# A convolution by two-stage transforms and an MLP on one core: first inverse stage in 64x32 tiles, its shuffles to 32 partitions, four rows with the last pair read in place, filter chunk on other partitions, new order

## The chip, the core and the metric

The kernel runs on one core of one Trainium2 chip. A core has TensorE (PE in the profile; its weight loads are PEld), VectorE (DVE), ScalarE (ACT), GpSimd (POOL), SyncE (SP), which here only issues DMAs, and 16 DMA engines. The metric is the device time of one execution in microseconds; lower is better.

## What is computed

The input is x = A_q, 2048 positions by 448 channels in bfloat16. Two sublayers follow each other, each on a layer norm and with a residual. Cut to what matters:

```python
def _A_ref(q, k, v, shift_k, ssm_k, ssm_D):
    k_shift = sum(k_pad[:, t:t + S, :] * shift_k[:, ks - 1 - t] for t in range(ks))   # 4 taps
    kv = k_shift * v
    y = irfft(rfft(kv, padded to 2 * S) * rfft(ssm_k, padded to 2 * S))[:S]           # along positions
    return q * (y + kv * ssm_D)

def _B_ref(x, w1, b1, w2, b2):
    h = _layernorm(x)
    u = _gelu(einsum("bsd,sf->bdf", h, w1) + b1)      # mixes the 2048 positions
    return (einsum("bdf,fs->bds", u, w2) + b2).transpose(0, 2, 1)

h = x + _A_ref(_layernorm(x), A_k, A_v, ...)
out = h + _B_ref(_layernorm(h), B_w1, B_b1, B_w2, B_b2)
```

## The kernel before

Everything lies in one SBUF array, `arena`; the parts of it are reused from stage to stage. Position 16 q + r is kept on partition q in row r, so a tensor is 128 partitions by 16 rows by 448 channels. The long convolution is a transform of 4096 points in two stages forward, a product, and two stages back, each stage a set of small matmuls with constant tables.

The steps are named in the order table: *loads* and *con* (inputs and tables), *kT* (the filter, which comes as channels by positions in four chunks of 128, 128, 128 and 64 channels, is transposed on TensorE, line 1086), *kv* (transposes of k, line 988, the four-tap filter as matmuls with diagonal weights, line 1014, and the product with v on VectorE, line 1053), *k1* and *u1* (first forward stage of the filter and of kv, line 1114, four tiles of 32 columns; each result goes from PSUM to SBUF on ScalarE or VectorE, line 1130, and two of them are then shuffled from SBUF to SBUF by a DMA, line 1134), *k2* and *u2* (second forward stage, line 1154), *i1* (products and first inverse stage), *i2* (second inverse stage, line 1324, with the gate, the residual and the layer norm of each row), *mlp* (lines 1455, 1465 and 1476), and fillers on TensorE (*dummy*, *warm*, line 1235). *q* and *xn* are the first layer norm's statistics.

The forward tables of the second stage, FW, are made on GpSimd: four operations of line 888, each over the whole table, spread one small table (c_fw) by a mask. GpSimd also casts the taps (line 968) and makes the diagonal weights DG from them (line 973). A k2 or u2 matmul needs all four spreads.

The inverse stage works in eight pairs jj. VectorE makes two products of 128 by 1792 (line 1183) into a ring of four buffers. For each half h of the pair 16 matmuls of 64 by 64 tiles (line 1200) fill two PSUM banks, and as soon as a half is done its evacuation (line 797 on ScalarE) brings it to TU. Then two shuffles (line 1225) bring the pair to TZ, where each lands on 16 partitions in steps of eight:

```python
TZ[jj:jj + 121:8, 8 * s:8 * s + 8].rearrange("p r c d -> p r (c d)")   # <- TU[:, 2 * jj + s]
```

The order of the pairs is 6, 0, 1, 5, 4, 2, 3, 7. The last pair's shuffles are smaller (lines 1212 and 1218, two of them issued by GpSimd), because rows 0 and 1 read that pair in TU itself: the constant NZ is 2, their place in TZ is filled with zeros (line 1166, a DMA), and each has two more matmuls with a table EW (line 1330). All other rows wait for the last pair's shuffles.

The order of every engine's instructions is written out in the table ORDER, a string per engine of steps and numbers of operations in them; a planner in the kernel walks through it, gives out PSUM banks and sets semaphores. An engine runs its list strictly in order: what waits holds up all that is behind it. SyncE's list is the order of the DMAs on its queue.

## Time and profile before

| | |
|---|---|
| runs | 175.47 us median of 3 (174.85 to 177.84) |
| profiled execution | 176.85 us, its span 174.8 us |
| granted TensorE clock, mean | 0.99 |
| busy: PE, DVE, ACT, POOL | 161.4, 91.6, 84.4, 36.5 us |
| moved by DMA | 36.87 MB, 211 GB/s on average |

The span is what the trace covers, from the first to the last instruction; the rest of the execution's time lies around it. The page lists busy times, the chain of work that ended last, and groups of instructions by line. A row of the timeline gives start, length, engine, line, operation, shapes and count, and in brackets the idle time before it with what ended it. A row of the chain gives start, length and what. In the rows of DMA issues the last number is the time from issue to landing in microseconds. Stages, by the timeline: filter transposes 4.7 to 11.9, k1 from 12.3, taps 23.9 to 33.8, second stage from 35.5, products 53.3 to 72.2, first inverse stage to 73.3, second inverse stage from 77.3, MLP from 84.4 to the end.

### The profile page before, as it was taken

The numbers are of one execution on the slowest core, as the hardware profiler recorded it, in microseconds if no ns is written. First come the engines' busy times: TensorE is split into PE (matmuls) and PEld (weight loads), VectorE is DVE, ScalarE is ACT, GpSimd is POOL, SyncE is SP. The second block draws the span as 40 slices with busy tenths as digits, with TensorE's granted clock in tenths as the row PEclk, the third lists the DMA queues.
The fourth block names the chain that finished last, engine by engine and source line by source line (L and its number), as shares of the span: only waits on it lengthen the run. The fifth ranks groups of instructions, "written<-read, shape, count | busy, mean of one in ns | idle before, by whom it ended". The sixth has DMA issues, their size and how long they took to land.

```text
span 174.8 us, 3713 instructions
## 1 busy us (share of the span) xinstructions
PE 161.4 (92%) x1565; PEld 95.8 (55%) x1565; DVE 91.6 (52%) x170; ACT 84.4 (48%) x128; POOL 36.5 (21%) x67
## 2 busy tenths in 40 slices
PE   6889999879977899949999999999999999999994
PEld 2666886533323444413444555555567777777783
DVE  0249889969987999938888730000002232231232
ACT  3239994869987999953968522622120000000000
POOL 1006917900000000234588750000000000000000
PEclk9999999999999999987999999999999999999999
DMA  5999989977885569895999999960000111101111
GB/s 184 283 324 407 366 265 306 401 204 286 291 302 164 194 190 213 220 193 94 385 389 406 416 420 424 413 273 0 0 0 4 53 53 53 42 14 53 53 53 53
DMA packets 16702, 36.87 MB, mean 211 GB/s; under 512 B 2349, under 2 KB 10206, under 8 KB 16686
## 3 DMA queue, kind: packets, MB, share of 16 engines
q1 hardware_dynamic: 16446, 36.47, 61.4%
q8 instruction: 12, 0.20, 0.5%
q0 software_dynamic: 96, 0.09, 0.3%
q10 hardware_dynamic: 144, 0.08, 0.2%
q14 instruction: 4, 0.03, 0.1%
HBM read 23.79 MB, written 1.84 MB: 147 GB/s over the span
## 4 chain that ended last, share of the span: by engine, by line
PE 71%; DMA 15%; ACT 7%; DVE 3%; SPq 2%; issue 1%; DVEq 0%
PE ps L1476 24%; PE ps L1455 12%; PE ps L1465 12%; DMA arena<-arena 11%; PE ps L1200 7%; PE ps L1114 5%; DMA arena<-in_A_ssm_k_dram 4%; PE ps L1324 3%; DVE arena L1183 2%; ACT arena L1130 2%; PE ps L988 2%; ACT arena L798 2%; PE ps L1014 2%; ACT arena L797 2%; PE ps L1154 2%; SPq L872 1%
## 5 line engine op out<-in xcount | busy, mean ns | idle before, releaser
L1476 PE MATMUL ps<-arena 128*128 128x448 bf16 (+2 forms) x238 | 42.7, 342 | 0.0
L1479 DVE SCALAR_TENSOR_TENSOR arena<-ps,arena 128x448 bf16<-128x448 f32 (+2 forms) x17 | 11.2, 657 | 57.5 <-PE ps L1476 57.4
L1476 PEld LDWEIGHTS ps<-arena 128*128 128x128 bf16 x238 | 33.3, 145 | 9.5
L797 ACT CAST arena<-ps 128x896 bf16<-128x896 f32 (+1 forms) x28 | 22.7, 921 | 1.8 <-PE ps L1154 1.7
L1130 ACT CAST arena<-ps 128x896 bf16<-128x896 f32 (+2 forms) x27 | 21.4, 843 | 4.2 <-PE ps L1114 4.0
L1455 PE MATMUL ps<-arena 128*128 128x448 bf16 x112 | 22.5, 353 | 0.0
L1465 PE MATMUL ps<-arena 128*128 128x448 bf16 x112 | 21.4, 352 | 0.0
L1154 PE MATMUL ps<-arena 128*64 128x448 bf16 x128 | 15.0, 359 | 3.7 <-DMA arena<-arena 2.0
L1445 ACT ACTIVATE arena<-ps,arena 128x448 bf16<-128x448 f32 x14 | 8.1, 643 | 20.5 <-PE ps L1465 14.3
L1183 DVE TENSOR_TENSOR arena<-arena 128x1792 bf16<-128x1792 bf16 x16 | 16.5, 1086 | 1.7 <-DMA arena<-arena 1.6
L1114 PE MATMUL ps<-arena 128*32 128x448 bf16 (+2 forms) x288 | 16.3, 335 | 0.4 <-ACT arena L798 0.3
L1455 PEld LDWEIGHTS ps<-arena 128*128 128x128 bf16 x112 | 10.7, 98 | 10.8 <-DVE arena L1408 1.0
L1465 PEld LDWEIGHTS ps<-arena 128*128 128x128 bf16 x112 | 11.0, 98 | 10.2
L1200 PE MATMUL ps<-arena 64*64 64x448 bf16 x256 | 13.7, 353 | 1.0 <-DVE arena L1183 0.5
L888 POOL TENSOR_SCALAR arena<-arena 128x1024 f16<-128x1024 f16 x4 | 11.4, 2851 | 13.3 <-DMA arena<-c_fw 13.3
L1154 PEld LDWEIGHTS ps<-arena 128*64 128x64 f16 x128 | 5.6, 108 | 12.4 <-ACT arena L797 2.8
L1200 PEld LDWEIGHTS ps<-arena 64*64 64x64 f16 x256 | 7.0, 106 | 7.3 <-ACT arena L797 3.1
L1324 PE MATMUL ps<-arena 128*128 128x448 bf16 x32 | 8.5, 375 | 2.6 <-DMA arena<-arena 2.5
L1269 POOL TENSOR_SCALAR arena<-arena 128x4 f32<-128x4 f32 (+1 forms) x5 | 1.3, 266 | 45.4 <-DVE arena L1263 45.3
L800 DVE COPY arena<-ps 128x1024 bf16<-128x1024 bf16 (+1 forms) x10 | 6.3, 654 | 8.0 <-PE ps L1086 8.0
L1114 PEld LDWEIGHTS ps<-arena 128*32 128x32 f16 x288 | 7.3, 95 | 5.5 <-ACT arena L798 1.5
L1378 ACT ACTIVATE arena<-arena 128x448 bf16<-128x448 bf16 x14 | 8.0, 572 | 4.2 <-DVE arena L1349 3.9
(61 smaller groups left out, 170.9 us busy)
## 6 DMA issues: line engine op xcount, KB each, us to landing
arena<-arena SPq DMA_DIRECT2D x16, 448.0 KB, 5.3
arena<-in_B_w_dram SPq DMA_DIRECT2D x8, 896.0 KB, 10.1
arena<-in_B_w_dram SPq DMA_DIRECT2D x2, 2048.0 KB, 17.5
arena<-arena SPq DMA_DIRECT2D x14, 224.0 KB, 4.2
arena<-in_B_w_dram SPq DMA_DIRECT2D x2, 1536.0 KB, 19.3
arena<-in_A_k_dram SPq DMA_DIRECT2D x4, 448.0 KB, 7.5
arena<-in_A_q_dram SPq DMA_DIRECT2D x4, 448.0 KB, 5.8
arena<-in_A_v_dram SPq DMA_DIRECT2D x4, 448.0 KB, 8.8
```

The source lines that it names most:

```text
L797: return e.copy(out=dst(), in_=src())
L888: return e.tensor_scalar(out=dst, in0=FC, scalar1=MK[:, k:k + 1], scalar2=None, op0=ALU.mult)
L1114: op("pe", lambda e, W, quad=quad, r=r, q=q, x=x, c0=c0, d0=d0, dw=dw: e.matmul(quad(x, q), E0[:, 128 * x + c0:128 * x + c0 + 32], src[:, ...
L1130: return e.copy(out=dst, in_=u) if W == "act" else e.tensor_copy(out=dst, in_=u)
L1154: op("pe", lambda e, W, b=bs[h], h=h, j=j, c=c, par=par: e.matmul(PS[64 * par:64 * par + 64, b.slots[c], 0:D], FW[:, 2 * j + h, 64 * c:64 ...
L1183: op("dve", lambda e, W, m=m, i=i: e.tensor_tensor(out=MR(m.slots[0]).rearrange("p (x y) d -> p x y d", x=2), in0=TU[:, i].unsqueeze(2).br ...
L1200: k = op("pe", lambda e, W, b=bs[h], m=ms[h], par=par, t=t, tab=tab, xy=xy, s=s, o=o: e.matmul(PS[64 * o:64 * o + 64, b.slots[s], 0:D], ta ...
L1324: k = op("pe", lambda e, W, b=b, r=r, h=h: e.matmul(Pb(b), ET[:, 2 * r + h, :], TZ[:, slot[r], h, :], start=(h == 0), stop=(h == 1 and r > ...
L1455: op("pe", lambda e, W, r=r, fc=fc, b=bs[fc]: e.matmul(Pb(b), W1A[:, r, 128 * fc:128 * fc + 128], Q[:, r, :], start=(r == 0), stop=(r == R ...
L1465: op("pe", lambda e, W, r=r, fc=fc, b=b: e.matmul(Pb(b), W1B[:, r, 128 * (fc - n0):128 * (fc - n0) + 128], Q[:, r, :], start=(r == 0), sto ...
L1476: op("pe", lambda e, W, r=r, fc=fc, b=b, d0=d0, d1=d1: e.matmul(Pb(b)[:, d0:d1], W2[fc // 7][:, fc % 7, r:S:R], G[:, fc, d0:d1], start=(fc ...
L1479: op("dve", lambda e, W, r=r, b=b, d0=d0, d1=d1: e.scalar_tensor_tensor(out=X[:, r, d0:d1], in0=Pb(b)[:, d0:d1], scalar=bm[:, r:r + 1], in ...
```

## The change

**First inverse stage.** The tiles are 64 rows by 32 columns: 64 matmuls a pair instead of 32, each with 32 columns of weights, and the two halves of a pair meet in the same four PSUM banks. So both evacuations of a pair follow its last matmul. A bank now holds, in its four partition quarters, the four sums of the pair for the same rows, and a shuffle lands on 32 partitions in steps of four:

```diff
-                        for s, par in ((0, 0), (0, 1), (1, 0), (1, 1)):
-                            o = par ^ s
-                            k = op("pe", lambda e, W, b=bs[h], m=ms[h], par=par, t=t, tab=tab, xy=xy, s=s, o=o: e.matmul(
-                                PS[64 * o:64 * o + 64, b.slots[s], 0:D], tab[64 * par:64 * par + 64, 64 * s:64 * s + 64],
...
+                        for g in range(4):
+                            for par in range(2):
+                                qd = (2 * h + par) ^ g
...
+                                    PS[32 * qd:32 * qd + 32, bs[g >> 1].slots[g & 1], 0:D],
+                                    tab[64 * par:64 * par + 64, 32 * g:32 * g + 32],
...
-                        TZ[jj:jj + 121:8, 8 * s:8 * s + 8].rearrange("p r c d -> p r (c d)"),
-                        TU[:, 2 * jj + s].rearrange("p c d -> p (c d)")),
...
+                            TZ[off:off + 125:4, c, 8 * g:8 * g + 8].rearrange("p (a b) d -> p a (b d)", b=2), view(o_u, [2 * D])),
```

Here c is jj >> 2 and off is jj & 3; TZ has its two halves apart (`[2, R, D]` instead of `[R, 2, D]`). The table for this stage is half as large.

**Last pair.** Rows 0 to 3 (NZ is 4) read it in TU, with one more matmul each. Its first shuffle carries rows 4 to 7 alone (128 runs of 896 bytes), its second is whole; both are issued by SyncE. The zeros are written by GpSimd (line 1155 of the changed kernel) and not by a DMA. Rows 4 to 7 wait for the first of the two shuffles, rows 8 to 15 for the second.

```diff
-                        for h in range(2):
-                            k = op("pe", lambda e, W, b=b, r=r, h=h: e.matmul(
-                                Pb(b), EW[:, 2 * r + h, :], TU[:, R - 1, h, :], start=False, stop=(h == 1)),
...
+                        k = op("pe", lambda e, W, b=b, r=r: e.matmul(
+                            Pb(b), EW[:, r, :], view(o_TU + (4 * (R // 2 - 1)) * DB, [D]), start=False, stop=True),
```

**Filter.** The chunk of 64 channels is loaded to partitions 32 to 95 instead of 0 to 63, into a buffer that VectorE fills with zeros before, and is transposed like the others with 128 rows. The load waits for the fill.

```diff
+            op("dve", lambda e, W: e.memset(KN[:, 3, :], 0.0), w=[(o_KN + 4096 * 3, 4096)], est=620.0)
...
-                op(Dq, lambda e, W, c=c: e.dma_start(KN[0:CW[c], c, :], A_ssm_k[128 * c:128 * c + CW[c], :]),
...
+                op(Dq, lambda e, W, c=c: e.dma_start(KN[KP[c]:KP[c] + CW[c], c, :], A_ssm_k[128 * c:128 * c + CW[c], :]),
```

**Gate.** The gate's value of rows 4 and up is written to the ring of product buffers instead of over TZ.

**Order.** ORDER is new for all engines. Of one engine's string, as an example, three rows of SyncE's:

```diff
-        "xload.3:0 i1.14:36 i1.14:35 i1.1:36 i1.1:35 i1.4:35 i1.4:34 i1.12:35-36 i1.10:36 i1.10:35 i1.6:36 i1.6:35 "
...
+        "i1.1:67-68 i1.14:67-68 i1.8:68 i1.8:67 i1.10:68 con.8:0 i1.10:67 i1.12:67-68 i1.6:67-68 i1.4:66-67 w1a.0:0 "
+        "i1.16:67-68 w1a.1:0 w1a.2:0 w1a.3:0 w1b.0:0-3 w2.0:0-3 mlp.25:15 mlp.27:15 mlp.29:15 mlp.31:15 mlp.33:15 "
```

The pairs come as 0, 6, 3, 4, 5, 2, 1, 7. Lines are those of each kernel: the changed kernel's 900, 860, 911, 921, 918, 906, 903, 928 and 914 are loads (filter, constants, k, biases, D, taps twice, x, v).

SyncE at the start, of the changed kernel, from the fourth DMA on; ahead of it are one filter chunk, the identity and the 64-channel chunk.

```order
L900 DMA arena<-in_A_ssm_k_dram 128x2048 x2
L911 DMA arena<-in_A_k_dram 128x1792
L921 DMA arena<-in_B_b_dram 14x128
L860 DMA arena<-c_e 128x256
L860 DMA arena<-c_fw 128x1032
L918 DMA arena<-in_A_ssm_D_dram 1x448
L911 DMA arena<-in_A_k_dram 128x1792 x2
L906 DMA arena<-in_A_shift_k_dram 64x4
L911 DMA arena<-in_A_k_dram 128x1792
L903 DMA arena<-in_A_shift_k_dram 128x3x4
L928 DMA arena<-in_A_q_dram 128x1792
L906 DMA arena<-in_A_shift_k_dram 64x4
```

The 64-channel chunk has moved from behind the other three to ahead of two of them; c_fw stands before most of k instead of behind the first x load; the last piece of the taps (the second row of 906) stands behind all of k and one load of x.

GpSimd before, from the first table spread (line 888) on, and then the same place of the changed kernel (spread 876, cast of the taps 960, diagonal weights 965, zeros 1155; 1269 and 1254 belong to the layer norm and wait for VectorE):

```order
L888 TENSOR_SCALAR arena<-arena 128x64x16
L968 CAST arena<-arena 128x16
L973 TENSOR_TENSOR arena<-arena 128x1024
L888 TENSOR_SCALAR arena<-arena 128x64x16
L1269 TENSOR_SCALAR arena<-arena 128x2
L888 TENSOR_SCALAR arena<-arena 128x64x16
```

```order
L960 CAST arena<-arena 128x16
L876 ISA
L876 TENSOR_SCALAR arena<-arena 128x64x16
L965 TENSOR_TENSOR arena<-arena 128x1024
L876 TENSOR_SCALAR arena<-arena 128x64x16 x2
L1236 MEMSET arena 128x2
L876 TENSOR_SCALAR arena<-arena 128x64x16
L1155 MEMSET arena 128x4x448
```

The cast now stands ahead of the first spread, and the layer norm's operations behind the last. On TensorE the first k2 group comes, before, when all of line 1014 is done; in the changed kernel four k2 groups stand behind the fourth of its eight steps and after the last k1 group.

SyncE at the end of the inverse stage, before and then changed (1225 and 1209 are shuffles of pairs, 1212, 1218 and 1204 smaller ones of the last pair, 1428 and 1413 quarters of the first half of W1, 860 and 872 tables):

```order
L1428 DMA arena<-in_B_w_dram 128x4x896
L1166 DMA arena<-arena 16x4x448
L936 DMA arena<-in_A_q_dram 128x1792
L1225 DMA arena<-arena 16x8x896 x14
L1212 DMA arena<-arena 16x8x448 x2
L1218 DMA arena<-arena 8x6x448 x2
L872 DMA arena<-c_et 128x1024
```

```order
L1209 DMA arena<-arena 32x4x896 x7
L860 DMA arena<-c_ew 128x512
L1209 DMA arena<-arena 32x4x896 x7
L1413 DMA arena<-in_B_w_dram 128x4x896
L1204 DMA arena<-arena 32x4x448
L1209 DMA arena<-arena 32x4x896
L1413 DMA arena<-in_B_w_dram 128x4x896 x3
```

The first quarter of W1 has moved from ahead of all inverse shuffles to between pair 1 and the last pair, 7.

TensorE in the second inverse stage of the changed kernel (1220 warm, 1310 the stage's two matmuls a row, 1315 the in-place ones, 1440 MLP): the nine matmuls up to the second 1315 need nothing of the last pair's shuffles; the next, row 7's second one, does.

```order
L1220 MATMUL ps<-arena 128x448
L1310 MATMUL ps<-arena 128x448 x2
L1315 MATMUL ps<-arena 128x448
L1310 MATMUL ps<-arena 128x448 x5
L1315 MATMUL ps<-arena 128x448
L1310 MATMUL ps<-arena 128x448
L1315 MATMUL ps<-arena 128x448
L1310 MATMUL ps<-arena 128x448 x7
L1220 MATMUL ps<-arena 128x448
L1315 MATMUL ps<-arena 128x448
```

Before, rows 0 and 1 came first with four matmuls each, and all others behind the last pair's shuffles.

130 lines of the change are left out of this document (58 added, 72 removed), and 103 rows, old and new, of the table ORDER.

## Prediction

> **What bounds the kernel now.** I read the page's engine shares first, then the chain of waits in order of time, then the stretches of the windows view in which the chain stands on a DMA.
>
> ```profile
> PE 161.4 (92%) x1565; PEld 95.8 (55%) x1565; DVE 91.6 (52%) x170; ACT 84.4 (48%) x128; POOL 36.5 (21%) x67
> ```
>
> TensorE is busy for 92% of the span, but that is a mean over three parts. The chain shows them:
>
> ```profile
> 3.83 6.81 DMA arena<-in_A_ssm_k_dram
> ...
> 10.69 1.18 PE ps L1086 x16
> ...
> 23.97 2.39 PE ps L1014 x74
> ...
> 47.14 6.11 DMA arena<-arena
> ...
> 53.33 1.10 DVE arena L1183
> ...
> 74.30 6.35 DMA arena<-arena
> ...
> 80.70 0.75 PE ps L1324 x2
> ```
>
> From 80.70 on TensorE hardly stops (the 84 to 104 row below is 20.00 of 20), and the change leaves that work as it is: whatever makes it run through earlier than 80.70 comes off the end one for one. Before it there are three places where something else is last: the filter's last chunk (landing at 10.64), the last forward shuffle (landing at 53.25, and VectorE's first product behind it), and the last inverse shuffle (landing at 80.65). In the windows view (engine columns, granted clock, DMA share, GB/s) the first and the third look alike:
>
> ```profile
> 8.00:10.00 2.00, 1.22 (x16) 1.08 (x16) 0.00 (x0) 0.60 (x2) 0.00 (x0) 1.00 1.00 196
> 14.00:20.00 6.00, 6.00 (x138) 4.46 (x138) 5.95 (x13) 5.69 (x9) 5.24 (x4) 1.00 1.02 410
> 65.00:68.00 3.00, 3.00 (x60) 1.48 (x54) 3.00 (x4) 3.00 (x5) 0.00 (x0) 1.00 0.97 206
> 73.00:79.00 6.00, 3.73 (x19) 1.57 (x16) 3.24 (x9) 3.81 (x7) 2.40 (x3) 0.89 1.11 199
> 78.00:81.00 3.00, 2.76 (x8) 0.89 (x7) 1.77 (x4) 0.00 (x0) 1.28 (x2) 0.50 0.73 119
> 84.00:104.00 20.00, 20.00 (x106) 9.81 (x105) 15.01 (x47) 12.84 (x35) 15.18 (x38) 1.00 1.05 405
> ```
>
> The DMA engines are busy throughout (share about 1) yet move 196 to 206 GB/s while the 64-partition filter chunk or the inverse shuffles run, against 405 to 410 elsewhere. Half the rate is lost where few partitions are written.
>
> **The change part by part**, in times of the profiled execution.
>
> *Filter chunk.* It now lands on partitions 32 to 95 and is third in the queue. The filter and the identity are 1.88 MB; the queue had moved about 0.25 MB at 3.0, so at 400 GB/s the rest is through at 7.1 and landed at 8.2. Sixteen transposes of 1.18 us and the evacuation behind them: k1 can start at about 10; before, it came behind the transposes that ended at 11.87. The chunk has to wait for its zero fill, and with it SyncE and every load behind it.
>
> ```profile
> L1063 DVE MEMSET arena<- 128x448 bf16 x1 | 0.4, 432 | 0.9 <-PEq L1524 0.9
> ```
>
> The fill of 2048 columns starts behind this one at 1.3 and takes between 0.5 us (hardly more than for 448) and 2.0 (in proportion). The load would go out at 1.6; up to 1.4 us of delay lie behind the 524 KB already queued, so 0 to 0.8 us are left: I take 0.2. From there to the first filter-gate matmul (L1014 at 23.97) TensorE was busy without a gap (the 14 to 20 row) and has the same work less one k1 group: 21.7. Term: −2.3 us.
>
> *Where that lead goes.* The new order puts four k2 groups on TensorE right behind k1's last group, ahead of half the L1014 matmuls. k2 needs all four table spreads of GpSimd:
>
> ```profile
> 14.67 2.85 POOL L888 TENSOR_SCALAR arena<-arena 128x1024 f16<-128x1024 f16 x1 [13.32 <-DMA arena<-c_fw]
> 17.48 0.19 POOL L968 CAST arena<-arena 128x16 f32<-128x16 bf16 x1
> 17.76 1.90 POOL L973 TENSOR_TENSOR arena<-arena 128x1024 bf16<-128x1024 bf16 x1
> 32.35 2.86 POOL L888 TENSOR_SCALAR arena<-arena 128x1024 f16<-128x1024 f16 x1
> 35.47 0.95 PE L1154 MATMUL ps<-arena 128*64 128x448 bf16 x8 [1.16 <-POOL arena L1281]
> 7.74 0.47 SPq L914 DMA_DIRECT2D arena<-in_A_shift_k_dram  x1
> arena<-in_A_shift_k_dram SPq DMA_DIRECT2D x1, 0.5 KB, 7.0
> ```
>
> Before, the fourth spread ended at 35.2, since VectorE's statistics stood between them, and TensorE waited 1.16 us for it (the row names the small operation just behind it). Now the four follow each other, but the L968 cast stands ahead of all of them, and it needs the last shift-filter piece. Before, that landed at 14.7 (issued at 7.74, 7.0 us), behind some 3.6 MB; now it is behind 4.5 MB, at full rate about 15.2. So 15.2 + 0.2 + 4 × 2.85 + 1.9 + 0.3 = 29.0. TensorE gets to k2 after half of L1014 (208 matmuls at 2.39 us for 74, so 3.4 us), two k1 groups and a warm matmul: 21.7 + 4.5 = 26.2. It waits 2.8 us, and the rest of L1014 waits behind it, with VectorE's multiplies and nearly all of ScalarE's evacuations behind that. From 29.0 ScalarE has 20 evacuations to the last u1 group.
>
> ```profile
> 45.75 0.90 ACT L1130 CAST arena<-ps 128x896 bf16<-128x896 f32 x1
> 54.29 19.92 ACT L797 CAST arena<-ps 128x896 bf16<-128x896 f32 x24 [1.23 <-PE ps L1154]
> 70.08 2.08 DVE L1183 TENSOR_TENSOR arena<-arena 128x1792 bf16<-128x1792 bf16 x2
> arena<-arena SPq DMA_DIRECT2D x4, 448.0 KB, 3.1
> ```
>
> At 19.92/24 = 0.83 us each, and 0.7 us to the first, that is 46.3, with some waiting 46.8; before it was 46.65. The lead is used up: +0.1, between −1.5 (the piece lands at 13.5) and +1.5.
>
> *First product.* Before, the last u1 shuffle shared the queue with its neighbour and a table (6.11 us). Now ScalarE does two k2 evacuations and one of u1 between them, so it should land in 3 to 4 us (3.1 for one in an emptier queue). Then VectorE decides: four to five evacuations at 1.04 us stand ahead of the product, 51.6 against 53.33. Term, from 46.65: −1.8 us in all, from 0 to −3.
>
> *Products and first inverse stage.* On VectorE 16 products at 1.03 and two evacuations follow in both kernels: 18.8 us, last product at P = 70.4 instead of 72.16. TensorE has 512 matmuls of 32 columns instead of 256 of 64:
>
> ```profile
> 59.70 3.22 PE L1200 MATMUL ps<-arena 64*64 64x448 bf16 x64 [0.49 <-DVE arena L1183]
> ```
>
> Four tiles side by side ran at 50 ns a matmul. If eight run side by side, it is 25 ns, and a pair of products takes 1.6 us as before, under the 2.08 that VectorE needs. The L1014 row shows 32 ns a matmul, weights included, so such a pace can be issued; from 25 to 32 the cost is 0 to 0.3 us at the end. I take 0.
>
> *The tail.* The pair's two evacuations now both wait for its last matmul: they end at P + 0.2 + 0.8 (32 matmuls) + 0.25 + 2 × 0.83 = P + 2.9 instead of about P + 2.05 (the shuffle of 74.30 follows them), which costs 0.85. Against this the shuffles write 32 partitions. Stage 1 shuffles of that pattern are part of the 410 GB/s row, so the backlog at half rate (73 to 79) should go. The Trainium skill, page "SBUF — State Buffer", section "Door 1: The DMA port swizzle", says that bits 2 to 4 and 6 of the partition choose the port: by that, steps of eight or partitions 0 to 63 reach 8 of 16 ports, and steps of four or 32 to 95 reach all. The slow rows agree; by the page the new rate would be double, no run here shows it yet.
>
> But the first quarter of W1 (896 KB) now stands on SyncE ahead of the last pair's two shuffles. What an 896 KB load does to a small transfer behind it, one place shows:
>
> ```profile
> 53.27 0.39 SPq L1428 DMA_DIRECT2D arena<-in_B_w_dram  x1
> 53.70 0.66 SPq L1166 DMA_DIRECT2D arena<-arena  x1
> arena<-in_B_w_dram SPq DMA_DIRECT2D x1, 896.0 KB, 4.9
> arena<-arena SPq DMA_DIRECT2D x1, 56.0 KB, 4.8
> arena<-arena SPq DMA_DIRECT2D x2, 224.0 KB, 3.3
> ```
>
> The 56 KB landed 0.3 us after the load. So: the pair before ends its evacuations at P + 0.85, its second shuffle takes SyncE half a microsecond, the load is issued at P + 1.45 and lands at P + 6.35, and the first piece of the last pair at P + 6.7, the second at P + 7.2; before, TensorE went on at 80.70 = P + 8.54. Rows 0 to 3 need only the shuffle before that, at P + 3.0, right behind the nine warm matmuls; nine of their matmuls run before TensorE stops at row 7. Term: −1.8 us. Bounds: +0.4 with a backlog as before, −3.5 if the last pair isn't held up (3.3 us from its issue at P + 2.2).
>
> *After that:*
>
> ```profile
> 77.28 0.57 PE L1324 MATMUL ps<-arena 128*128 128x448 bf16 x2 [2.27 <-DMA arena<-arena]
> 84.39 1.11 PE L1455 MATMUL ps<-arena 128*128 128x448 bf16 x5
> ```
>
> 17 matmuls stand between TensorE's restart and the first MLP matmul (L1455), against 17 before in 84.39 − 80.70 = 3.7 us, the first of them at half clock: −0.2, if VectorE's queue (rows 2 and 3 are combined before row 0 is normalised) isn't later than TensorE.
>
> **Sum:** −1.8 (first product) − 1.8 (tail) − 0.2 = −3.8 us: span 171.0. The profiled execution took 176.85 for its span of 174.8; the runs shown have a median of 175.47, and I take the difference from that: **171.7 us**, by itself 169 to 174.
>
> **Rivals.**
>
> *The last pair isn't held by the W1 load* (0.18). For it: shuffles of 224 KB landed in 3.3 us. Against: the 56 KB row. Then TensorE hardly stops: −1.7 more, 170.0.
>
> *The lead is lost in idle stretches* (0.25). TensorE now stands idle about 2.8 us at k2 and 1.8 us before row 7. After the 2.3 us idle before 77.3 the clock was 0.50 for 3 us (the 78 to 81 row); there a DMA was last anyway. Once after k2 it costs 1.5 us, and the table pieces may land 1 us later: 174.1. The same if the shuffles stay near 200 GB/s, with the W1 load on top of their backlog: 174. Against: 1.5 us gaps elsewhere left the clock at 1.00.
>
> *Eight tiles don't run side by side* (0.17). If the two row halves take turns, the pace stays 50 ns: 512 matmuls are 25.6 us, from 4.5 us after the first product, and the stage ends 30.1 us after it instead of 19.8: +10.3, 182.0. TensorE decides from (19.8 − 4.5)/512 = 30 ns on; at 37 ns all of the gain is gone, at 44 the kernel is 2% slower. Against it: four tiles already share banks in pairs at 50 ns. The Trainium skill, page "TensorEngine Tiling (Array Packing)", section "Restrictions and Gotchas", says that different row tiles cannot access the same PSUM bank at the same time. By that rule the pace would be this rival's; but the 64x64 tiles also write one bank from both row halves, and at 50 ns for 448 columns they do not take turns, so the trace speaks against it.
>
> **How the numbers follow.** The forecast has 0.40, the first rival 0.18: faster by over 2% (about what a measurement of this kernel can tell from no change) 0.58; within 2% 0.25; slower 0.17. The range for 8 in 10 takes in the first two rivals with the bounds of the front, and the third up to 41 ns: 168.0 to 177.5.
>
> **What would show it.** Right: filter transposes over by 10; a TensorE wait on GpSimd of 2 to 3 us before k2 near 26 to 29; last product near 70; DMA near 400 GB/s in the inverse stage; the first MLP matmul near 80.5. Wrong: L1189 matmuls above 30 ns, the last shuffle landing over 7.5 us behind the last product, or a clock of 0.50 after k2.

## The result, and the profile after

The changed kernel is slower: 181.24 us median (179.44 to 181.38) against 175.16 for the kernel before, ratio 1.034 (95% interval 1.025 to 1.043). The forecast had 171.7 us, with 177.5 at the upper end of its range. The profiled execution took 181.38 us for a span of 179.4.

The chain of waits of the changed kernel in order of time (start, length, what):

```profile
8.80 6.29 DMA arena<-in_A_shift_k_dram
15.09 0.03 POOLq L558
15.12 1.72 issue
...
17.12 2.86 POOL arena L876
...
21.86 5.65 POOL arena L876 x2
...
27.55 2.83 POOL arena L876
...
30.73 1.70 PE ps L1144 x8
...
50.11 5.22 DMA arena<-arena
...
55.35 1.09 DVE arena L1170
...
68.92 0.43 PE ps L1189 x8
69.36 1.71 ACT arena L795 x2
...
79.02 4.99 DMA arena<-arena
```

Where the kernel before had the filter's chunk and TensorE's own work at the front, GpSimd's table spreads now stand on the chain up to 30.4. What holds them up is the last piece of the taps. The chain puts the end of GpSimd's wait down to another piece (landing at 15.09) and calls the rest "issue", but the small cast behind it waits for three pieces. The last went out at 9.97, and the slower of line 906's two pieces took 6.8 us:

```profile
9.97 0.47 SPq L906 DMA_DIRECT2D arena<-in_A_shift_k_dram  x1
DMA to landing us min/median/max: 6.2/6.5/6.8
```

So it landed at 16.81 (the trace has the last sixteenth of it there), and GpSimd went on at 16.86. In the inverse stage TensorE and ScalarE take turns. The last shuffle (79.02) still ends it, in 5.0 us instead of 6.4.

The timeline of the same kernel shows what each place costs:

```profile
21.96 1.62 PE L1006 MATMUL ps<-arena 64*128 64x256 bf16 x44 [0.19 <-issue]
30.73 1.70 PE L1144 MATMUL ps<-arena 128*64 128x448 bf16 x8 [3.77 <-POOL arena L876]
32.47 1.73 ACT L796 ACTIVATE arena<-ps 128x896 bf16<-128x896 f32 x2 [5.05 <-PE ps L1144]
34.12 1.29 DVE L1045 TENSOR_TENSOR arena<-ps,arena 128x512 bf16<-128x512 f32 x2 [5.15 <-PE ps L1006]
69.34 1.71 ACT L795 CAST arena<-ps 128x896 bf16<-128x896 f32 x2 [0.47 <-PE ps L1189]
71.53 1.71 ACT L795 CAST arena<-ps 128x896 bf16<-128x896 f32 x2 [0.47 <-PE ps L1189]
78.09 1.71 ACT L795 CAST arena<-ps 128x896 bf16<-128x896 f32 x2 [0.47 <-PE ps L1220]
84.06 0.36 PE L1310 MATMUL ps<-arena 128*128 128x448 bf16 x1 [2.49 <-DMA arena<-arena]
88.97 1.31 PE L1440 MATMUL ps<-arena 128*128 128x448 bf16 x5
```

The filter gate starts at 21.96, 2.0 us ahead of before (forecast 21.7). Then TensorE stands 3.77 us in front of k2, and ScalarE and VectorE over 5. In the inverse stage a pair of evacuations comes every 2.19 us, each time after 0.47 us of waiting; before, 24 evacuations followed each other without a gap (the row of 54.29 in the prediction). The first MLP matmul comes at 88.97 instead of 84.39.

The windows of the changed kernel (engine columns, granted clock, DMA share, GB/s):

```profile
31.00:36.00 5.00, 5.00 (x80) 3.04 (x80) 1.37 (x3) 2.78 (x4) 0.00 (x0) 0.74 0.43 150
81.00:84.00 3.00, 0.57 (x3) 0.10 (x1) 1.55 (x4) 0.83 (x3) 0.00 (x0) 1.00 0.97 355
84.00:88.00 4.00, 3.94 (x13) 1.75 (x14) 1.60 (x5) 2.63 (x5) 0.55 (x1) 0.60 0.55 157
```

The clock is 0.74 behind the wait at k2 and 0.60 behind the wait at 84. These are means over the windows: in the trace's record of the clock it is 0.50 from 30.19 to 33.60 and from 84.80 to 88.21, and 1.00 around that. The 355 GB/s are of W1 and the last pair together; what the new placement does to the shuffles alone, e5 shows below.

In every run of this study the part from the first MLP matmul to the end takes 90.2 to 90.5 us. So a run is three lengths: up to the first product, from there to the end of the last inverse evacuation (the stage), and from there to the first MLP matmul (the tail). All times are from the timelines; ratios are to runs of the kernel before of the same series, with 95% intervals. They leave out runs over 1.5% above the fastest of the same kernel, so that e2's rests on three of ten runs, e5's on two of four, and e16 with one run left has none; the profiled executions of these three are among those left out.

| run | ratio | first product | stage | tail | first MLP |
|---|---|---|---|---|---|
| before | 1 | 53.33 | 20.9 | 10.2 | 84.39 |
| forecast | | 51.6 | 21.7 | 7.3 | 80.6 |
| changed | 1.034 (1.025 to 1.043) | 55.35 | 24.5 | 9.2 | 88.97 |
| e1 all spreads first | 1.011 (1.003 to 1.019) | 53.34 | 24.4 | 9.2 | 86.92 |
| e14 two spreads first | 0.996 (0.992 to 1.001) | 51.43 | 24.6 | 7.9 | 83.86 |
| e15 filler matmuls | 1.018 (1.014 to 1.022) | 54.63 | 24.9 | 7.8 | 87.32 |
| e2 W1 early | 0.999 (0.992 to 1.006) | 56.56 | 24.4 | 5.1 | 85.98 |
| e3 other order of matmuls | 1.023 (1.015 to 1.031) | 55.63 | 23.4 | 8.3 | 87.35 |
| e4 64x64 tiles | 1.011 (1.003 to 1.019) | 55.65 | 21.2 | 9.5 | 86.41 |
| e16 fewer signals | | 56.47 | 22.1 | 9.9 | 88.40 |
| e7 = e1 + e2 + e3 | 0.998 (0.993 to 1.003) | 54.69 | 23.4 | 5.9 | 84.05 |
| e11 = e1 + e2, third order | 1.000 (0.996 to 1.005) | 53.32 | 23.7 | 5.9 | 82.88 |
| e13 = e14 + e2, third order | 0.974 (0.970 to 0.978) | 50.06 | 23.8 | 5.5 | 79.41 |
| e17 = e14 + e2 + e16 | 0.975 (0.968 to 0.982) | 51.87 | 22.0 | 5.2 | 79.12 |
| e19 = e17, fewer signals in the gate | 0.964 (0.959 to 0.968) | 52.18 | 21.4 | 5.7 | 79.22 |
| e9 old order of the front | 1.039 (1.027 to 1.051) | 50.27 | 32.0 | 9.8 | 91.99 |
| e6 before, filter chunk moved | 1.002 (0.997 to 1.007) | 52.12 | 22.0 | 10.1 | 84.16 |
| e5 before, 32-partition shuffles | 0.988 (0.981 to 0.995) | 52.98 | 20.9 | 10.2 | 84.09 |
| e18 before, fewer signals | 1.001 (0.997 to 1.005) | 53.70 | 20.8 | 9.7 | 84.19 |

### The profile page after: what moved, and what is told of

The parts are those of the page before. It is cut to its first block, busy times and chain, and to the rows that moved or that the text cites. A ratio compares the mean times of both kernels' runs of the same rounds, so it can differ in the third digit from the quotient of the medians.

```text
span 179.4 us, 4212 instructions
## 1 busy us (share of the span) xinstructions
PE 164.7 (92%) x1821; PEld 102.3 (57%) x1821; DVE 94.9 (53%) x175; ACT 84.2 (47%) x125; POOL 36.7 (20%) x66
## 4 chain that ended last, share of the span: by engine, by line
PE 62%; DMA 9%; ACT 9%; POOL 7%; DVE 5%; SPq 3%; issue 2%; POOLq 0%; DVEq 0%
PE ps L1461 23%; PE ps L1440 12%; PE ps L1450 12%; POOL arena L876 6%; DMA arena<-arena 6%; PE ps L1189 5%; ACT arena L795 4%; DMA arena<-in_A_shift_k_dram 4%; PE ps L1310 3%; ACT arena L1120 3%; PE ps L1144 2%; ACT arena L796 2%; PE ps L1006 2%; PE ps L1220 1%; DVE arena L798 1%
## 5 line engine op out<-in xcount | busy, mean ns | idle before, releaser
L795 ACT CAST arena<-ps 128x896 bf16<-128x896 f32 (+1 forms) x28 | 23.2, 889 | 5.0 <-PE ps L1189 3.7
L1440 PE MATMUL ps<-arena 128*128 128x448 bf16 x112 | 22.8, 353 | 0.0
L1450 PE MATMUL ps<-arena 128*128 128x448 bf16 x112 | 21.4, 353 | 0.0
L1120 ACT CAST arena<-ps 128x896 bf16<-128x896 f32 (+2 forms) x24 | 19.2, 868 | 3.9 <-PE ps L1104 3.1
L1144 PE MATMUL ps<-arena 128*64 128x448 bf16 x128 | 15.6, 372 | 5.3 <-POOL arena L876 3.8
L1430 ACT ACTIVATE arena<-ps,arena 128x448 bf16<-128x448 f32 x14 | 8.2, 640 | 19.8 <-PE ps L1450 14.4
L1170 DVE TENSOR_TENSOR arena<-arena 128x1792 bf16<-128x1792 bf16 x16 | 17.1, 1087 | 0.6 <-PE ps L1189 0.3
L1189 PE MATMUL ps<-arena 64*32 64x448 bf16 x512 | 16.0, 349 | 1.5 <-ACT arena L795 0.9
L1189 PEld LDWEIGHTS ps<-arena 64*32 64x32 f16 x512 | 12.4, 90 | 5.1 <-ACT arena L795 2.2
L1045 DVE TENSOR_TENSOR arena<-ps,arena 128x512 bf16<-128x512 f32 (+1 forms) x16 | 9.2, 616 | 7.1 <-PE ps L1006 7.0
L1310 PE MATMUL ps<-arena 128*128 128x448 bf16 x32 | 9.5, 404 | 2.5 <-DMA arena<-arena 2.5
L796 ACT ACTIVATE arena<-ps 128x896 bf16<-128x896 f32 x10 | 8.9, 916 | 5.9 <-PE ps L1144 5.8
L1120 DVE CAST arena<-ps 128x896 bf16<-128x896 f32 (+2 forms) x12 | 10.4, 884 | 1.0 <-PE ps L1104 0.8
## 6 DMA issues: line engine op xcount, KB each, us to landing
arena<-in_B_w_dram SPq DMA_DIRECT2D x2, 1536.0 KB, 18.8
```

Of the source, the lines that this page charges most:

```text
L795: return e.copy(out=dst(), in_=src())
L796: return e.activation(out=dst(), in_=src(), func=ACT.Copy, scale=scale)
L1120: return e.copy(out=dst, in_=u) if W == "act" else e.tensor_copy(out=dst, in_=u)
L1144: op("pe", lambda e, W, b=bs[h], h=h, j=j, c=c, par=par: e.matmul(PS[64 * par:64 * par + 64, b.slots[c], 0:D], FW[:, 2 * j + h, 64 * c:64 ...
L1170: op("dve", lambda e, W, m=m, i=i: e.tensor_tensor(out=MR(m.slots[0]).rearrange("p (x y) d -> p x y d", x=2), in0=TU[:, i].unsqueeze(2).br ...
L1189: k = op("pe", lambda e, W, bs=bs, m=ms[h], par=par, t=t, tab=tab, xy=xy, g=g, qd=qd: e.matmul(PS[32 * qd:32 * qd + 32, bs[g >> 1].slots[g ...
```

## The experiments

The first theories were: A, the inverse stage's hand-over of PSUM banks between TensorE and ScalarE holds the loss; B, the wait for the spreads does; C, the last pair behind the load of W1 and the half clock do.

### The front: e1, e14, e15

e1, GpSimd's order in ORDER:

```diff
-"kv.0:1 q.0:1 loads.14:0 kv.0:2 kv.0:0 con.5:0 kv.0:3 con.3:0 con.4:0 q.0:0 con.6:0 zero.0:0
+"kv.0:1 q.0:1 loads.14:0 con.5:0 con.3:0 con.4:0 con.6:0 kv.0:2 kv.0:0 kv.0:3 q.0:0 zero.0:0
```

Expected: 

> Edit: on GpSimd the four table spreads (L876) go ahead of the small cast that waits for the last shift-filter piece (L960); nothing else. Measured so far: before 175.2 us, changed 181.2 us. Theory B (the wait for the spreads in front of k2, 3.77 us and half clock behind it, shifts all that follows): the wait before k2 is gone, u1's last evacuation ends at about 47 instead of 50.1, the first product starts at about 52.5 instead of 55.35, and the end moves by the same 2 to 3.5 us: 178 to 179. Theory A (the loss sits in the hand-over of the first inverse stage): the front may move as much, but the last evacuation of the stage stays 5.1 us behind the last product; if the front's move is lost before the first product, the time stays at 181.

The timeline of e1:

```profile
11.32 11.33 POOL L876 TENSOR_SCALAR arena<-arena 128x1024 f16<-128x1024 f16 x4 [10.06 <-DMA arena<-c_fw]
22.93 1.91 POOL L965 TENSOR_TENSOR arena<-arena 128x1024 bf16<-128x1024 bf16 x1
24.98 1.62 PE L1006 MATMUL ps<-arena 64*128 64x256 bf16 x44 [1.67 <-ACT arena L795]
```

The spreads could run from 11.3 on, and the wait before k2 is gone. But the diagonal weights (L965), which the filter gate needs, now come last and are done at 24.84, and the gate starts at 24.98 instead of 21.96. (The row names an evacuation that ended within 0.1 us of them; in e7 and e11, with the same order on GpSimd, the chain goes through L965.) The first product gains 2.0 us, the stage nothing: B holds, and a part of it is hidden by the edit's own price. In e14 the gate is not late.

```diff
+"kv.0:1 q.0:1 loads.14:0 con.5:0 con.3:0 kv.0:2 kv.0:0 kv.0:3 con.4:0 con.6:0 q.0:0 zero.0:0
```

Expected: 

> The changed kernel with GpSimd's order alone edited: two table spreads ahead of the cast that waits for the last shift-filter piece, the other two behind it. With all four ahead, the wait before k2 was gone, but the filter table (L965) was done only at 24.9 and the first filter-gate matmul moved from 21.96 to 24.98, so only 2.0 us of the first product came back. With two ahead: cast at 17, filter table at 19.2, last spread at 24.9, TensorE reaches k2 at 26.2 to 27 and doesn't wait. If the wait before k2 and its half clock are what pushed the first product from the predicted 51.6 to 55.35, it starts at 50.5 to 51.7 now, and the end moves by 3.5 to 4.5 us: 177. If ScalarE's and VectorE's evacuations behind it set the pace, the first product stays near 53.3: 179.

The timeline of e14:

```profile
10.85 5.69 POOL L876 TENSOR_SCALAR arena<-arena 128x1024 f16<-128x1024 f16 x2 [9.59 <-DMA arena<-c_fw]
21.62 1.61 PE L1006 MATMUL ps<-arena 64*128 64x256 bf16 x44
28.25 0.95 PE L1144 MATMUL ps<-arena 128*64 128x448 bf16 x8 [1.62 <-DMA arena<-arena]
51.43 1.09 DVE L1170 TENSOR_TENSOR arena<-arena 128x1792 bf16<-128x1792 bf16 x1 [0.18 <-DMA arena<-arena]
80.40 0.36 PE L1310 MATMUL ps<-arena 128*128 128x448 bf16 x1 [2.64 <-DMA arena<-arena]
```

TensorE waits 1.62 us here for a shuffle of k1, not for GpSimd; the first product starts at 51.43, and the clock stays at 1.00. The order of these GpSimd operations is worth 3.9 us at the first product, the largest single term. At the first MLP matmul it is 5.1 (88.97 to 83.86), but 1.3 of that is the tail, where TensorE stood no shorter than in the changed kernel (2.64 us against 2.49) and the clock did not fall this time; the edit doesn't touch that.

How much of that is the half clock? e15 leaves the waits and fills them:

```diff
-"... kv.13:22-27 k2.5:0-3 ... i2.10:0 i2.47:1 ..."
+"... kv.13:22-27 warm.14:0 ... warm.30:0 k2.5:0-3 ... i2.10:0 warm.31:0 ... warm.41:0 i2.47:1 ..."
```

Expected: 

> The changed kernel with 28 more warm matmuls (no result used): 17 in the wait before k2, 11 in the wait for the last pair's landing. The waits stay as long as they are; only the clock behind them should stay at 1.00 instead of 0.50 to 0.74. If the half clock has a price of its own (the theory: 0.75 us on the k2 matmuls and about as much on the filter gate behind them, 1.2 us behind the restart), the first product comes at 54 to 54.6 instead of 55.35 and the end 1.5 to 2.7 us earlier: 178.5 to 179.7. If it only fills time in which something else is last, or if the clock falls all the same: 181.

Windows of e15, to hold against 0.74 and 0.60 above, and its first k2 group:

```profile
31.00:36.00 5.00, 4.82 (x86) 2.71 (x84) 1.93 (x5) 3.35 (x5) 0.13 (x1) 1.00 0.52 175
84.00:88.00 4.00, 3.97 (x21) 1.70 (x19) 3.09 (x11) 3.71 (x9) 1.48 (x4) 1.00 0.62 178
31.49 0.95 PE L1144 MATMUL ps<-arena 128*64 128x448 bf16 x8
```

The clock is 1.00 in both places. The tail is 1.4 us shorter. The first product comes only 0.7 us earlier, but k2 started 0.76 later here, since the last piece of the taps landed at 17.57 instead of 16.81. From the start of k2 to the first product it is 23.1 us in e15 and 24.6 in the changed kernel, so the half clock cost 1.5 us there. The other profiled runs with the new front order bear this out: 23.1 to 23.4 where the clock was 1.00 behind k2's start (e1, e7, e11, e13, e14, e17, e19), 24.8 to 25.8 where it fell (e2, e3, e4, e16). Work whose result nobody uses makes the kernel 1.6% faster (1.018 against 1.034); the half clock has a price of its own, as expected.

### The tail: e2

```diff
-"... i1.4:66-67 w1a.0:0 i1.16:67-68 ..."
+"w1a.0:0 i1.1:67-68 ... i1.4:66-67 i1.16:67-68 ..."
```

Expected: 

> Edit: on SyncE the first quarter of W1 (896 KB) is issued before the inverse stage's first shuffle, as in the kernel before, instead of in front of the last pair's two shuffles. Theory C (the last pair lands behind that load, TensorE stands 2.5 us before row 7 and restarts at half clock): the last pair lands 2.5 to 3 us behind its issue, TensorE restarts at about 82 instead of 84.06 and the end moves by 2 to 3 us: 178.5 to 179.5. Theories A and B: what precedes the tail is as long as before, so no more than the 2 us between landing and restart can be won, and if the load then delays the stage's first shuffles, nothing: 180 to 181.

The timeline of e2 at the place where TensorE stood 2.49 us, and the window behind its wait at k2:

```profile
82.33 0.35 PE L1315 MATMUL ps<-arena 128*128 128x448 bf16 x1
82.52 0.35 PE L1310 MATMUL ps<-arena 128*128 128x448 bf16 x1
31.00:36.00 5.00, 5.00 (x46) 2.61 (x44) 1.29 (x2) 1.73 (x2) 0.00 (x0) 0.50 0.43 147
```

The wait is gone and with it the half clock behind it; the tail falls from 9.2 to 5.1 us. In this execution the clock at k2 was worse (0.50 in the whole window), and the first product came 1.2 us later, so the first MLP matmul gains 3.0 us in all. C holds for the tail. The median of all ten runs is 178.28 us, a little under the 178.5 to 179.5 expected. W1's early load did not delay the stage (24.4 us, 24.5 in the changed kernel).

### The stage: e3, e4, e7, e11, e13

A said that a bank group comes free only after 64 matmuls, the way to ScalarE and two evacuations: 4.3 us for two pairs. e3 lets the first two banks finish first:

```diff
-for h in range(2):
-    for t, (tab, xy) in enumerate(...):
-        for g in range(4):
+for gp in range(2):
+    for t, (tab, xy) in enumerate(...):
+        for h in range(2):
+            for g in (2 * gp, 2 * gp + 1):
```

Expected: 

> Edit: the 64 matmuls of a pair in another order, so that the 32 that write the first two banks end before the 32 that write the other two; a bank pair is then evacuated while the other half still runs. Same matmuls, same count, same result. Theory A (only two pairs fit into PSUM, and a bank group is free again only after 64 matmuls 1.96 us + 0.65 us to ScalarE + two evacuations 1.71 us = 4.3 us for two pairs, 2.19 us a pair against 2.08 us of products; behind the last product come 0.2 + 1.96 + 0.65 + 1.71 us): the pair falls to 2.08 to 2.1 us, the last evacuation ends 3.5 to 4 us behind the last product instead of 5.1, and the end moves by 1 to 2 us: 179 to 180. Theories B and C: the front and the tail are the same, so 181.

The timeline of e3:

```profile
71.30 1.87 PE L1189 MATMUL ps<-arena 64*32 64x448 bf16 x64 [0.32 <-DVE arena L1170]
75.95 0.91 ACT L795 CAST arena<-ps 128x896 bf16<-128x896 f32 x1 [0.19 <-PE ps L1189]
77.05 0.91 ACT L795 CAST arena<-ps 128x896 bf16<-128x896 f32 x1 [0.19 <-PE ps L1189]
```

The evacuations now come singly, and TensorE waits for products instead of banks, but an evacuation comes every 1.10 us: a pair still takes 2.19. Only the end is shorter (stage 23.4), since one evacuation instead of two follows the last matmuls; the shorter tail (8.3 us) goes with a clock that stayed at 1.00. The time, 180.98 us, missed the 179 to 180 expected. The hand-over was not what set the pace. e4 halves the number of matmuls:

```diff
-for g in range(4):
-    for par in range(2): ... PS[32 * qd:32 * qd + 32, bs[g >> 1].slots[g & 1], 0:D]
+for s in range(2):
+    for par in range(2): ... PS[64 * o:64 * o + 64, bs[h].slots[s], 0:D]
```

Expected: 

> Edit: the first inverse stage with 64x64 tiles, 32 matmuls a pair, in the changed kernel's order and with its evacuations and shuffles; the values land in other rows (the placement that the 64x32 tiles gave is left out), sizes and counts of everything else are the same. If the narrow tiles' pace is what costs (31 ns each instead of 25): TensorE takes 1.58 us a pair instead of 1.96, the loop over the banks is 1.58 + 0.65 + 1.71 = 4.0 us for two pairs, so products set the pace again, and the last evacuation ends 3.3 to 4 us behind the last product: 179.5. If it is the bank hand-over, and not the pace: this gains less than the other order of the matmuls. Theories B and C: 181.

```profile
64.97 9.07 DVE L1170 TENSOR_TENSOR arena<-arena 128x1792 bf16<-128x1792 bf16 x9
73.18 1.71 ACT L795 CAST arena<-ps 128x896 bf16<-128x896 f32 x2 [0.29 <-PE ps L1189]
75.18 1.71 ACT L795 CAST arena<-ps 128x896 bf16<-128x896 f32 x2 [0.29 <-PE ps L1189]
```

In the timeline of e4 nine products run without a gap, a pair takes 2.0 us and the stage 21.2. So the loss goes with the 64x32 tiles; whether by their number or by their width, this run can't tell. Three combined runs tried orders again, with the load of e2 and the front of e1 (e7, e11) or e14 (e13). e7 has e3's order; e11 and e13 the first product's 32 matmuls, then the second's by banks:

```diff
+for h, gs in ((0, (0, 1, 2, 3)), (1, (0, 1)), (1, (2, 3))):
+    for t, (tab, xy) in enumerate(...):
+        for g in gs:
```

e7, expected: 

> The changed kernel with the three single edits together: spreads ahead of the cast, first quarter of W1 issued before the first inverse shuffle, and the 64 matmuls of a pair ordered so that the first two banks are done after 32. Alone they moved the ratio to before from 1.034 to 1.011, 0.999 and 1.023. If the three losses follow each other in time, they add up: about 0.965, 170 us. If W1 delays the shuffles when both run early, or if the front's gain is lost at the products, 0.98 to 0.99: 172 to 174.

e11, expected: 

> As the run with the three edits together, but with another order of a pair's matmuls: the 32 of the first product over all four banks, then the 16 of the second product for the first two banks, then the 16 for the other two, so only four different tiles follow each other in the second half. If the 31 ns a matmul are what TensorE needs to issue 64x32 tiles with their weights, the pair still takes 1.96 us, the products' ring comes free after 32 matmuls, products run at 2.08 us a pair again, and the last evacuation ends about 3 us behind the last product: 0.5 to 1 us below the other combined run. If tiles must be eight different ones to overlap, the second half runs at 47 ns or more, the pair takes 2.5 us, TensorE sets the stage's pace and it ends 2 to 4 us later than in the other combined run.

e13 (with e14's front), expected: 

> That GpSimd order, with the first quarter of W1 issued before the first inverse shuffle, and the pair's matmuls with the first product's 32 first and then the two halves of the banks one after the other. The same with all four spreads ahead had its first product at 53.32, the last evacuation at 77.0, the first MLP matmul at 82.88 and a span of 173.3 (90.4 us follow the first MLP matmul in every run so far). If the front's 2 us come through: first MLP matmul at 81, span 171.4, 172.5 to 174 us, ratio 0.985 to 0.99. If TensorE (33 ns a matmul, 512 of them) or ScalarE sets the stage's pace from its own start, less than 1 us of it comes through: ratio 0.995 to 1.

The gains did not add up in e7 (0.998, not 0.965): e1's front costs the gate 3 us, and the stage stayed at 23.4. e11 is no faster than e7 in the ratio, though its first MLP matmul came 1.2 us earlier in the profiled execution; e7's has a stretch of half clock behind the wait for the gate (25.86 to 29.27), e11's has none. In e13 the front's gain comes through at last: 172.09 us against 176.45, ratio 0.974. Its stage, from the timeline:

```profile
58.98 13.18 PE L1188 MATMUL ps<-arena 64*32 64x448 bf16 x384
```

13.18/384 = 34.3 ns a matmul with no wait left, where 25 had been forecast. This row alone doesn't say why: in this order the second product's matmuls have only four different tiles side by side, and four ran at 50 ns in the kernel before.

### What sets the pace: e16 and its control e18

The rows of single instructions and the trace's record of TensorE's completion count, both of the changed kernel around 69 us, tell more than the grouped views:

```
starts of L1189 matmuls: 68.924 68.928 68.931 68.934 68.938 68.941 68.944 68.948  (8 within 0.02 us)
                         69.123 69.128 ... 69.147   69.313 ... 69.336   69.502 ... 69.532
completion count goes up at: ... 69.220 69.254 69.288 69.323 69.357 69.391 69.425 69.459 ...
ScalarE's evacuation of the fourth pair starts at 69.345; the count reaches 257
(four pairs of 64 and one warm matmul) at 69.323
the kernel before, L1200, four tiles: count goes up at 60.061 60.095 60.129 60.163
                                                       60.250 60.284 60.318 60.353 ...
```

Eight tiles start together, and from the second eight on each eight 189.5 ns after the one before: 23.7 ns a matmul. But each of these matmuls also signals that it is done, and the count goes up by one every 34.15 ns without a break. ScalarE starts 0.02 us after the pair's count is reached, long after its last matmul. 64 x 34.15 ns = 2.19 us. The kernel before shows the same distance inside each four, and a pause of 87 ns behind it, so there the count kept up. In e16 only the last of eight matmuls signals:

```diff
+    def issue(self, W, ins, quiet=False):
+        if quiet:
+            return _Ev(0, W, self.cnt[W] + 1)      # who waits for it waits for the next that signals
...
+                                sch.ops[k].quiet = not (g == 3 and par == 1)
```

Expected: 

> The changed kernel; in the first inverse stage only the last of every eight matmuls signals that it is done (8 signals a pair instead of 64), whoever waited for one of the others waits for the next one that signals. Theory S (TensorE's completions go out one per 34.15 ns, and 64 of them make 2.19 us a pair): matmuls start 24 ns apart all through, a pair takes the products' 2.05 to 2.1 us, ScalarE's pairs of evacuations follow without the 0.47 us gaps, the last evacuation ends 3 to 3.5 us behind the last product instead of 5.0, and the end moves by 2 to 2.7 us: 178.5 to 179.3, ratio 1.02. Theory I (issuing a weight load and a matmul takes 34 ns): the pair stays at 2.19 us and the time at 181.

The timeline of e16:

```profile
64.94 7.35 PE L1193 MATMUL ps<-arena 64*32 64x448 bf16 x257 [0.44 <-DVE arena L1174]
65.81 9.07 DVE L1174 TENSOR_TENSOR arena<-arena 128x1792 bf16<-128x1792 bf16 x9
75.21 3.33 ACT L799 CAST arena<-ps 128x896 bf16<-128x896 f32 x4 [1.20 <-PE ps L1193]
```

257 matmuls in 7.35 us are 28.6 ns each, and TensorE now keeps up with the products, which run without a gap at 1.01 us. The count goes up once per 189 ns, eight matmuls at a time. The stage is 22.1 us instead of 24.5, a gain within the 2 to 2.7 expected; the last evacuation ends 3.7 us behind the last product (expected 3 to 3.5). At the first MLP matmul only 0.6 us of it is left in the profiled execution: its first product was 1.1 us later (the last piece of the taps landed late, as in e15), and its tail 0.7 longer. The four runs took 176.05 and 179.87 to 180.73 us, where 178.5 to 179.3 had been expected. 176.05 is the one with a mean granted clock of 1.00; e15, with all signals and the clock at 1.00 in all its runs, took 179.1 to 180.7. Theory S holds for the stage; for the whole time that one run is all there is.

Control e18, the kernel before with the same edit for its 64x64 tiles. Expected: 

> Control: the kernel before with the same edit (of four matmuls of its inverse stage only the last signals). 32 signals of 34 ns are 1.1 us a pair, under the 2.08 of the products, and ScalarE's evacuations there have no gap. Theory S: no change, ratio 0.995 to 1.005. If fewer signals help whatever the stage: as much faster as the other run.

Measured 1.001 (0.997 to 1.005), stage 20.8 against 20.9: 32 signals a pair are 1.1 us and were hidden. With e4 (32 matmuls, all signals) and e16 (64 matmuls, 8 signals) this leaves the signals as the cause, and not the number of matmuls.

e17 joins e14, e2 and e16. Expected: 

> The changed kernel with two spreads ahead of the cast and two behind, W1's first quarter early, and fewer signals in the inverse stage; the matmuls in the change's own order. With the reordered matmuls and all signals this was 172.1 us, first MLP matmul at 79.41. Theory S: first product at 50 to 51.4, last evacuation 3 to 3.5 us behind the last product, first MLP matmul at 77.5 to 78.5, span 168 to 169, 170 to 171 us, ratio 0.965. Theory I: the stage is as slow as in the run with the GpSimd order alone (last evacuation 5.0 us behind the last product), first MLP matmul at 80, 172.5.

171.37 us against 176.44, ratio 0.975 (0.968 to 0.982), stage 22.0, first MLP matmul at 79.12. It misses the expected 77.5 to 78.5: in the last pair TensorE stands another 0.9 us that the profile gives as "issue", and rows 4 to 15 follow each other without a wait from 74 on, so the tail is work. e13, without the edit, has the same time; its front was 1.8 us ahead in the profiled execution.

e19 adds the filter gate. Expected: 

> As that, and in the filter gate too (L1006, 208 matmuls of 64 to 256 columns, 33 to 36 ns apart) only the last matmul of each accumulation signals. Theory S: its matmuls of 64 columns run at 27 ns or less, the gate's 208 take 5.5 to 6 us instead of 7; TensorE reaches k2 about 0.5 us earlier, and where ScalarE and VectorE are last there, nothing more comes of it: 0 to 0.7 us below the run without it. Theory I: the gate's matmuls keep their pace and the time is the same.

The timeline of e19:

```profile
23.31 1.61 PE L1010 MATMUL ps<-arena 64*128 64x256 bf16 x44
25.35 1.90 PE L1010 MATMUL ps<-arena 64*128 64x64 bf16 x58
```

The gate's matmuls keep their pace to the hundredth (1.62 and 1.90 before), so there theory I is right: their pace is not the signals'. 170.77 us against 176.44, ratio 0.964 (0.959 to 0.968). The trace shows nothing that the edit gained over e17 (first MLP matmul at 79.22 and 79.12), so the difference is not credited to it. e13, e17 and e19 beat both kernels.

### Parts alone: e9, e6, e5

e9 is the changed kernel with the old order of steps up to the second inverse stage. Expected: 

> The changed kernel with the order of the kernel before up to the second inverse stage (filter edit kept; loads, k1, k2, u1, u2, products, spreads in the old order; both evacuations of an inverse pair next to each other; the load of W1's first quarter where the changed kernel has it). Separates front from inverse stage. Theory A (the stage and its tail hold the loss, 4.6 - 2.0 = 2.6 us of it): first product at 51.5 to 53.3, last evacuation still 5 us behind the last product, 177.5 to 179. Theory B (the new front order is all of it): no slower than the kernel before, 174 to 176.

The timeline of e9:

```profile
60.76 0.36 PE L1189 MATMUL ps<-arena 64*32 64x448 bf16 x1 [1.69 <-ACT arena L795]
61.56 4.91 PE L1189 MATMUL ps<-arena 64*32 64x448 bf16 x127 [0.45 <-ACT arena L795]
```

The first product comes at 50.27, the earliest of all but one, and yet the kernel is the slowest, with a stage of 32.0 us. In the old order u2 groups stand between the inverse pairs; a pair needs four banks at once, gets two, runs one matmul and waits for the others. Both expectations failed. In this order, then, the new stage needs the u2 groups ahead of it, and the time of the first product alone says little. (e9 also puts a pair's evacuations next to each other, so it isn't a pure reordering.)

e6 is the kernel before with the filter edit alone (its main lines; the placement and the transposes change as in the changed kernel):

```diff
+op("dve", lambda e, W: e.memset(KN[:, 3, :], 0.0), ...)
-"loads.0:0 con.0:0 loads.1:0 loads.2:0 loads.4:1 con.1:0 loads.3:0
+"loads.0:0 con.0:0 loads.3:0 loads.1:0 loads.2:0 loads.4:1 con.1:0
```

Expected: 

> The kernel before, with the filter edit alone: its last chunk on partitions 32 to 95 behind a zero fill, loaded third, transposed with all 128 partitions; every order table else as before. The changed kernel's first filter-gate matmul is 2.0 us earlier than before (21.96 against 23.97), yet with the spreads put first its first product stands at 53.34, where the kernel before has it (53.33). If the lead is lost by the new order behind it, it reaches the end here: filter gate at about 22 and 173 to 174 us against 175.5. If it is lost to the table spreads, whose fourth ends at 35.2 in the kernel before, or to ScalarE's and VectorE's evacuations: the same wait grows and the time stays within 0.7 us of before.

The gate starts 1.3 us earlier (22.64), the first product 1.2, and the last evacuation 0.15. The time is 1.002 (0.997 to 1.007). In the profiled execution the lead goes in one place:

```profile
53.50:57.00 3.50, 3.50 (x36) 1.48 (x36) 3.21 (x4) 3.02 (x4) 0.00 (x0) 0.51 0.98 328
57.66 16.41 ACT L797 CAST arena<-ps 128x896 bf16<-128x896 f32 x20 [1.02 <-PE ps L1204]
```

Behind a wait of 1.98 us for a shuffle the clock is at half (1.00 in the kernel before), and ScalarE waits 1.02 us for matmuls of the inverse stage. Runs of e6 with a mean granted clock of 1.00 are no faster than such runs of before (175.4 to 176.7 us against 174.7 to 176.4); where they lose the lead, no trace shows.

e5 is the kernel before with the inverse shuffles to 32 partitions (its main lines; the last pair's and the zeros' places change with it):

```diff
-TZ[jj:jj + 121:8, 8 * s:8 * s + 8]
+TZ[jj & 3:(jj & 3) + 125:4, 8 * s + 4 * (jj >> 2):8 * s + 4 * (jj >> 2) + 4]
```

Expected: 

> The kernel before with the inverse stage's shuffles written to 32 partitions in steps of four instead of 16 in steps of eight, sizes and issues unchanged (so the values land in other rows; the tables that fit this placement are left out). It has the shuffle's rate without the 64x32 tiles. If the rate of the shuffles is what the kernel before waits for at the end (206 GB/s at 65 to 68 us, landing 6.4 us after the issue), the windows show 350 to 400 GB/s, the last pieces land 3 to 4 us after their issue, TensorE goes on at 77.5 to 78.5 instead of 80.70, and the time is 2 to 3 us below before: ratio 0.985. If something else is last there (VectorE's and ScalarE's row work), it stays at 1.

A window of e5 and its DMA issues between 60 and 82 us (KB each, median us to landing; 4.2 for the kernel before):

```profile
65.00:68.00 3.00, 3.00 (x56) 1.45 (x48) 3.00 (x4) 3.00 (x5) 0.00 (x0) 1.00 0.53 205
arena<-arena SPq DMA_DIRECT2D x13, 224.0 KB, 2.3
```

The same 205 GB/s take a DMA share of 0.53 instead of 0.97, and a shuffle lands in 2.3 us. But TensorE goes on only 0.3 us earlier at the first MLP matmul: the first restart at 77.20 still waits, at half clock, and the rows' own work follows. The ratio, 0.988 (0.981 to 0.995), is near the expected 0.985, but it comes from runs of 173.52 and 175.36 us, and the profiled execution took 176.40, with a tail as long as before (10.2 us). So the trace does not show where the gain comes from; that stays open. What the trace does show is the room: the DMA engines need half the time for the same bytes. Its sign was the share and the time to landing; the 350 to 400 GB/s that were expected did not come (205, as before). The Trainium skill, page "SBUF — State Buffer", section "Door 1: The DMA port swizzle", which the forecast cites, says which bits of the partition choose a port; by it, steps of four reach twice the ports that steps of eight reach. The 0.53 against 0.97 agrees with it.

## Why the prediction was wrong

By the three lengths the forecast was short by 3.75 us at the first product, 2.75 in the stage and 1.9 in the tail: 8.4 us. Most of the rest up to 181.24 is its start: the terms are those of an execution of 176.85 us, and were taken off a median of 175.47.

- **Filter chunk: right in the sum.** The gate starts at 21.96 (21.7 forecast), the transposes end at 10.61 (by 10 forecast); the chunk's load went out at 2.42, not 1.6, since the zero fill held it up.
- **The wait before k2: right in place, wrong in size and in what it drags along.** This is the first step that failed: "at full rate about 15.2" for the last piece of the taps, and with it "It waits 2.8 us". The piece landed at 16.81. It went out at 9.97, and 6.8 us from issue to landing is what the forecast's own row for such a piece had shown (7.0). The last spread ended at 30.4, the wait was 3.77 us, and k2 started at 30.73 instead of 29.0: 1.7 us. Then the clock fell, which the forecast priced in a rival only (0.25, 1.5 us), and 1.5 is what it cost. From the start of k2 to the first product the forecast has 22.6 us; it was 24.6, and 23.1 in e15 with the clock at 1.00. That leaves 0.5 for the evacuations and the shuffle behind k2. In e14 the first product stands at 51.43, against the forecast's 51.6, but by some luck: k2 starts 0.75 us earlier than forecast there, and the way behind it is 0.6 longer.
- **Products and first inverse stage: the step "I take 0" failed.** Eight tiles do run side by side, 23.7 ns a matmul against 25 forecast. The Trainium skill, page "TensorEngine Tiling (Array Packing)", section "Restrictions and Gotchas", has it that different row tiles cannot use one PSUM bank at the same time; the starts above speak against it, since tiles of both row halves write the same four banks, on different partitions, within 0.02 us. But the pace that ScalarE sees is that of the completions, 34.15 ns. The views of before don't show it, as 32 of them a pair were hidden there; its trace's record of the count does. The forecast's own threshold ("TensorE decides from (19.8 − 4.5)/512 = 30 ns on") was met. The third rival named the right threshold for the wrong reason. From the first product to the end of the last the stage took 19.5 us instead of 18.8.
- **"P + 2.9": wrong,** and 2.1 of the stage's 2.75 us. The last evacuation ended 5.0 us behind the last product in the changed kernel, 3.7 with fewer signals. The forecast let half of the last pair's matmuls be done beforehand; with signals in arrears, none was: its first started at 75.48, the last product ended at 74.81.
- **The tail: mechanism right, price short.** The last pair lands behind the W1 load (4.99 us after its issue; forecast 4.5), and TensorE stops before row 7.
- **"After that": wrong by the clock.** From the restart to the first MLP matmul it is 3.5 us with the clock at 1.00, as forecast (e14: 80.40 to 83.86), but 4.9 in the changed kernel (84.06 to 88.97). The forecast took the half clock of before out of its sum (−0.2) and put none in behind the new stop, though it had the evidence in the row of 78 to 81.

All three signs that the forecast named for being wrong came: 1.96 us for 64 matmuls of L1189 (31 ns), the last pair's first piece landing 9.2 us behind the last product, and a clock of 0.50 after k2. So parts of two rivals came true on top of the forecast's own mechanism. Two of the faults are alike: a wait was costed at its length alone, without the clock behind it. The third is a rate, that of the signals, which the forecast did not look at.

## What to carry to other kernels

When a change doubles the number of small matmuls, look at the rate at which they report completion, not only at their pace: signal from the last matmul of a group alone. Price a new wait with what stands behind it, the clock included, and look for the few cheap operations ahead of it on the engine waited for; here a few GpSimd operations in another order were worth 3.9 us at the first product, as much as the whole change set out to win. Where an operation waits for several loads, look up when each landed, and don't take the one that the chain names for the last. Split a kernel at a point behind which nothing varies (here the first MLP matmul) and compare lengths between such points, not end times.
